# Attention, then a mixture of experts, on one core: choosing and turning the second slot of tokens earlier

## The chip, the core and the metric

The kernel runs on one core of a Trainium2 chip. The metric is device time in microseconds (us), the median of repeated runs. The engines are TensorE (PE; its weight loads are PEld), VectorE (DVE), ScalarE (ACT), GpSimd (POOL) and SyncE (SP). SP and POOL issue the DMAs.

## The reference

Eight batches of attention with twelve heads, 448 positions and a head of 64, scores capped by a tanh, in float32; then every token (3584 rows of 768) goes through the one of eight experts that its gate chooses.

```
scores = q @ k^T / sqrt(64)
scores = cap * tanh(scores / cap)
attn = softmax(scores)                    # over keys, with + 1e-9 in the sum
x = (attn @ v), heads side by side        # 3584 x 768
logits = x @ w_gate + modality_bias[modality_id]
e = argmax(logits, axis=1)
gate = softmax(logits)[e]
out[tokens of e] = gate * (relu(x @ w1[e]) @ w2[e])     # 768 -> 1024 -> 768
```

With the inputs as the reference draws them, expert 3 gets 1551 tokens (all of them in the first seven batches), expert 7 gets 1788 (1566 in the first seven) and expert 1 gets 245 (19); the others get none.

## The kernel before

*Attention.* The work is cut into 24 units of four heads, three to a batch, and each unit into seven steps of 64 keys. A step's scores are four matmuls; ScalarE takes tanh and exp; VectorE adds the exponentials up (tot); four more matmuls weigh v with them (xT). After a unit VectorE turns the result in blocks of 32 by 32 into token rows (tokens), and after a batch the rows, not yet divided by the softmax's sum, are stored to xd in device memory (store). Each row lies there in four quarters of 192 numbers.

*Routing.* After a batch, route finds each token's expert (oh), ranks it among its expert's tokens with two small matmuls (rank, from oh and from the running counts acc), and writes one entry of 16 numbers per token with indirect DMAs from POOL to the map, mapd, at row `expert * RG + rank` (L331). The entry holds the token, its gate weight, and two sets of six reciprocals of the softmax sums, each with the number of the row's quarter.

*Slots.* The experts' work is done in slots of 384 tokens (W) of one expert. A slot needs the expert's weights, its 384 map entries, and the rows that they name, gathered from xd into xg. The weights are float32 and are each split into a rounded part and the rest: ScalarE casts (ah, bh), VectorE subtracts (al, bl, L963), and each product is three matmuls. x is split in the same way (take, L987 and L988). A weight is loaded in blocks of 128 rows, through four buffers (raw) that are free again when VectorE has subtracted; w1 has six blocks, w2 eight.

*The first slot* is chosen from the counts after seven batches (early_slot): the first expert with at least 384 tokens. It is gathered, scaled and turned while the last batch is computed, and its first product is written out by hand together with the last batch's routing: hooks of ffn1 run after each block k and each column block f. The hook at ("k", 3) computes the last logits, the one at ("f", 3) ranks the last tokens, stores the last batch, and calls order().

*The other slots* are planned by slots() in order(), from the counts of all batches: a table (metai, copied to metad) with the expert and the map row of each full slot, and plani, which says how the rest ends. All of this is small VectorE instructions. FIXED planned slots run straight through; then one of four endings for the remainders.

*How a slot's x is made.* From the third slot on, quarter_rows reads the map in a layout in which each 32 partitions hold one quarter, quarter_index makes the row numbers (at), quarter_gather issues twelve indirect DMAs, and turn_rows lets VectorE scale and turn each 128 tokens into xt; take then splits xt. The second slot goes another way: rows() reads the map from SP as soon as metai is there, gather() issues three indirect DMAs, norm (L939) scales on VectorE, and TensorE turns xg by 18 transposes (move, L979) among the products of the first slot's ffn2.

What sets the order: instructions under pin keep the order of the program on their engine; the others are placed by the scheduler among them. Each engine works its row in order, so an instruction that waits holds up what stands behind it. In the first slot's ffn2 the products of the first 128 tokens go through the eight blocks of w2 once, both halves of a block together, and need bh and bl of that block.

Of the kernel before, what the change touches and what calls it, by code (L numbers as in the profile page):

```python
# [39 lines left out]
F32 = mybir.dt.float32  # L40
# [19 lines left out]
W = 384  # L60
# [12 lines left out]
FIXED = 7  # L73
# [18 lines left out]
class Program:  # L92
# [258 lines left out]
    def early_slot(self, pool, ps):  # L351

        nc = self.nc
        cnt = self.counts(pool, ps)
        sc = pool.tile([128, E], F32, name="esc")
        nc.vector.scalar_tensor_tensor(sc, cnt, float(W), self.desc, op0=ALU.is_ge, op1=ALU.mult)
        top = pool.tile([128, 1], F32, name="etop")
        nc.vector.tensor_reduce(top, sc, axis=AX.X, op=ALU.max)
        self.early = pool.tile([128, E], F32, name="early")
        nc.vector.tensor_scalar(self.early, sc, top, None, op0=ALU.is_equal)  # L360
        meta = pool.tile([128, 2], I32, name="emeta")
        for i, scale in enumerate((1.0, float(RG))):
            nc.vector.tensor_scalar(meta[:, i : i + 1], top, -scale, E * scale, op0=ALU.mult, op1=ALU.add)
        return meta

    def slots(self, pool, ps, early, then=None):
# [26 lines left out]
        if early:  # L393
            V.tensor_tensor(mask[:, :, 0], mask[:, :, 0], self.early, op=ALU.subtract)
            V.tensor_tensor(nbig, nbig, self.early, op=ALU.subtract)
# [6 lines left out]
        if early:  # L402
            V.tensor_tensor(start, base[:, :E], self.early, op=ALU.subtract)
        else:
            V.tensor_copy(start, base[:, :E])
# [76 lines left out]
    def attention(self, firsts, rp, xp):  # L482
        tc, nc = self.tc, self.nc
        pe, pin, V = nc.tensor, self.pin, nc.vector
        with ExitStack() as st:
# [330 lines left out]
            def last_ready():  # L816
                ready(5)
                turn2(SOON + 1)
                logits(SOON + 1)
                logits(SOON + 2)  # L820

# [15 lines left out]
            def last_rank():  # L837
                next(self.way, None)
                tokens(ND - 1)
                store(B - 1)  # L840
                soon(1)
# [47 lines left out]
    def quarter_rows(self, row, after=None):  # L889

        nc = self.nc
        r = self.register(nc.gpsimd, self.meta[row : row + 1, 1:2], NOROW, after)
# [29 lines left out]
    def quarter_gather(self, maps, n=TW):  # L922

        for g in range(n * 128 // FT):
            got = self.nc.gpsimd.indirect_dma_start(  # L925
                self.xg.rearrange("p t f -> p (t f)")[:, g * QW : (g + 1) * QW], None,
                self.xd.rearrange("n (q c) -> (n q) c", q=Q),
                bass.IndirectOffsetOnAxis(ap=maps[2][:, g : g + 1], axis=0),
                bounds_check=Q * NT - 1, oob_is_err=False,
# [306 lines left out]
    def run_slot(self, cur, n, ahead=None, raws=(), hooks=None, rows=None, few=False, index=None):  # L1236
# [24 lines left out]
        if hooks:  # L1261
# [3 lines left out]
            nxt[0], [lambda t=t: self.norm(nxt[1], t) for t in range(TW)] if hooks else (), quarters=bool(hooks)  # L1265
        )
        if nxt:
            if not hooks:
                for turn in turns:
                    turn()  # L1270
                then()
            pool = lambda k: (self.ps_h, "ph") if k % 3 == 2 else (self.ps_t, "ptr")
            moves = [
                lambda k=k: self.transpose(k, *pool(k)) if hooks else self.take(k, self.xt[:, k], nxt[2])
                for k in range(KC)
            ]
            if index:
                moves.insert(3, index)
# [5 lines left out]
    def run_slots(self, cur, hooks):  # L1284
# [4 lines left out]
        def rows(i, n=TW, more=True):  # L1289
            got = self.quarter_gather(maps[i], n)  # L1290
            if more:
                maps[i + 1] = self.quarter_rows(i + 1, got.ins)
# [6 lines left out]
        def ahead(i, n=TW):  # L1299
            if i == 0:  # L1300
                maps[0] = self.second
                maps[1] = self.quarter_rows(1, self.got)
            return self.expert(self.meta, i), maps[i], n

        for i in range(FIXED + 1):
            if i == FIXED:
                which = nc.values_load(self.plani[0:1, 2:3], min_val=0, max_val=len(ENDS))
            cur = self.run_slot(
                cur, TW, lambda: ahead(i), *((self.raws, hooks) if i == 0 else ()), rows=(lambda: rows(i)) if i else None,
                index=lambda: index(i + 1),  # L1310
# [143 lines left out]
    def build(self):  # L1454
        tc, nc = self.tc, self.nc
        with ExitStack() as st:
# [4 lines left out]
            with ExitStack() as sa:  # L1461
# [8 lines left out]
                with tc.If(big == 0) as branch:  # L1470
                    with ExitStack() as sb:
# [9 lines left out]
                        def order():  # L1481
                            self.meta = self.slots(rt, self.ps_r, True, hooks["last"])
                            self.second = self.rows(self.meta, 0)
                            self.got = self.gather(self.second).ins
# [68 lines left out]
```

## Time and profile before

| | |
|---|---|
| timed runs, median (three) | 802.48 us (800.44 to 803.19) |
| profiled execution, its own time | 795.47 us |
| its span, first to last instruction | 793.9 us |
| TensorE busy | 779.5 us, 98% |
| VectorE busy | 523.1 us, 66% |
| ScalarE busy | 502.2 us, 63% |
| POOL busy | 226.7 us, 29% |
| granted TensorE clock, mean | 0.998 of full |

The span begins with the first instruction and ends with the last; times in the rows below count from its start. Matmuls overlap in the pipeline, so a row's duration is longer than its distance to the next start. "Idle before" in square brackets is the time for which an engine waited ahead of an instruction, with what released it. Attention fills the first 300 us, the first slot's products run from 303 to 360 us, and the second slot starts there.

### The profile page before, as it was taken

Reading aid. Unit: us, or ns where it says so; the run is one execution under the profiler, and the core shown is the slowest. Engines: PE = TensorE matmul, PEld = TensorE weight load, DVE = VectorE, ACT = ScalarE, POOL = GpSimd, SP = SyncE. Lnnn points to the kernel's source line nnn. Section 1 sums busy time; section 2 is a strip of 40 time slices with the busy share of each in tenths; the row PEclk is TensorE's granted clock in tenths of the full one; section 3 lists DMA queues with packets and bytes.
Section 4 is the critical chain, followed back from the end, with each engine's and each line's share of the span. In section 5 each row is a group of like instructions: output and inputs, shape, how many; then the busy total and the mean of one; then the engine's idle time right before and its main releaser. Section 6 shows DMA issues by size and latency. Waiting matters only on the chain. (4 is left out here: it accounts for less than half of the span.)

```text
span 793.9 us, 15329 instructions
## 1 busy us (share of the span) xinstructions
PE 779.5 (98%) x5844; PEld 585.8 (74%) x5844; DVE 523.1 (66%) x875; ACT 502.2 (63%) x622; POOL 226.7 (29%) x258
## 2 busy tenths in 40 slices
PE   7999999999999999999999999999999999999996
PEld 3333333333333337999999999999999999999986
DVE  4688897888798898965826548265482664727830
ACT  6999999999999996354523545335443353537721
POOL 3000220022021150248180551814508146015202
PEclk9999999999999999999999999999999999999999
DMA  5466544362635565597445563465634645346772
GB/s 177 135 195 201 167 145 150 131 211 76 206 111 171 146 196 191 137 312 260 136 144 197 183 207 134 147 214 178 200 129 149 229 158 190 122 163 206 274 263 80
DMA packets 58787, 139.33 MB, mean 176 GB/s; under 512 B 9121, under 2 KB 25663, under 8 KB 58704
## 3 DMA queue, kind: packets, MB, share of 16 engines
q1 hardware_dynamic: 48224, 113.34, 44.1%
q0 software_dynamic: 10336, 24.91, 9.5%
q8 instruction: 48, 0.79, 0.4%
q14 instruction: 35, 0.29, 0.1%
q10 hardware_dynamic: 144, 0.00, 0.0%
HBM read 114.47 MB, written 24.34 MB: 175 GB/s over the span
## 5 line engine op out<-in xcount | busy, mean ns | idle before, releaser
L963 DVE TENSOR_TENSOR bl<-raw,bh 128x768 fp32r<-128x768 f32 x78 | 72.3, 956 | 121.8 <-ACT bh L962 120.6
L549 PE MATMUL xT<-pt,va 64*64 64x448 f32 x1344 | 151.5, 536 | 1.1 <-DVE xT L556 1.1
L521 ACT ACTIVATE pt<-sc 128x896 f32<-128x896 f32 x164 | 142.6, 906 | 10.4 <-PE sc L516 10.3
L1076 PE MATMUL py<-bh,hh 128*128 128x384 f32 x440 | 148.9, 339 | 0.1
L1076 PE MATMUL py<-bl,hh 128*128 128x384 f32 x440 | 148.3, 337 | 0.0
L1076 PE MATMUL py<-bh,hl 128*128 128x384 f32 x440 | 148.3, 337 | 0.0
L925 POOL DMA_INDIRECT xg<-xd,at x92 | 107.1, 1164 | 142.3 <-DVE at L908 114.0
L1022 PE MATMUL ph<-x,al 128*128 128x384 f32 (+1 forms) x456 | 147.3, 323 | 0.0
L524 ACT ACTIVATE pt<-pt 128x1792 f32<-128x1792 f32 x84 | 142.7, 1699 | 2.7
L537 DVE TENSOR_TENSOR tot<-tot,pt 128x896 f32<-128x896 f32 x118 | 127.9, 1084 | 11.0 <-ACT pt L524 6.4
L1018 PE MATMUL ph<-x,ah 128*128 128x384 f32 x360 | 120.6, 335 | 0.0
L1019 PE MATMUL ph<-x,ah 128*128 128x384 f32 x360 | 120.3, 334 | 0.0
L549 PEld LDWEIGHTS xT<-pt,va 64*64 64x64 f32 x1344 | 51.1, 133 | 76.2 <-issue 70.8
L331 POOL DMA_INDIRECT mapd<-pay,pos x32 | 36.3, 1134 | 233.4 <-DVE pos L324 185.8
L1098 ACT ACTIVATE ot<-py,mt 128x384 f32<-128x384 f32 x55 | 31.9, 580 | 107.4 <-PE py L1076 94.6
L1022 PEld LDWEIGHTS ph<-x,al 128*128 128x128 f32 x456 | 85.7, 188 | 0.0
L1033 ACT ACTIVATE hh<-ph 128x384 fp32r<-128x384 f32 x63 | 30.7, 491 | 85.3 <-PE ph L1022 81.4
L1076 PEld LDWEIGHTS py<-bh,hh 128*128 128x128 f32 x440 | 82.6, 188 | 1.0 <-ACT ot L1098 0.5
L516 PE MATMUL sc<-kq 64*64 64x448 f32 x672 | 79.5, 547 | 3.7 <-ACT pt L521 2.6
L1076 PEld LDWEIGHTS py<-bh,hl 128*128 128x128 f32 x440 | 82.6, 188 | 0.0
L1076 PEld LDWEIGHTS py<-bl,hh 128*128 128x128 f32 x440 | 82.6, 188 | 0.0
L516 PE MATMUL sc<-kx 64*64 64x448 f32 x672 | 78.6, 540 | 0.8 <-ACT pt L521 0.8
(248 smaller groups left out, 981.5 us busy)
## 6 DMA issues: line engine op xcount, KB each, us to landing
raw<-in_w_dram SPq DMA_DIRECT2D x81, 384.0 KB, 4.7
raw<-in_w_dram SPq DMA_DIRECT2D x48, 512.0 KB, 4.7
kq<-in_kq_dram SPq DMA_DIRECT2D x24, 448.0 KB, 4.2
va<-in_v_dram SPq DMA_DIRECT2D x24, 448.0 KB, 6.0
kx<-in_kq_dram SPq DMA_DIRECT2D x24, 448.0 KB, 4.0
xd<-xs SPq DMA_DIRECT2D x32, 336.0 KB, 7.1
raw<-in_w1q_dram SPq DMA_DIRECT2D x12, 512.0 KB, 6.5
mapd<-spare SPq DMA_DIRECT2D x4, 480.0 KB, 6.9
```

The costliest lines, as they stand in the source:

```text
L331: put = nc.gpsimd.indirect_dma_start(self.mapd, bass.IndirectOffsetOnAxis(ap=pos[:, c : c + 1], axis=0), pay[:, c, :], None, bounds_check= ...
L516: pin(pe.matmul(sc[i * KB : (i + 1) * KB, j, :S], kq[rows, s * KB : (s + 1) * KB], kq[rows, S:QK], start=True, stop=True,))
L521: pin(nc.scalar.activation(weights(n), sc[:, :, :S], AF.Tanh, scale=self.isc if slow else self.iscr))
L524: pin(nc.scalar.activation(pt, pt, AF.Exp, scale=self.cabsr))
L537: pin(V.tensor_tensor(tots[d], pt_of(n - 1) if s == 1 else tots[d], pt_of(n), op=ALU.add))
L549: pin(pe.matmul(self.xT[j * D : (j + 1) * D, i, :S], vas[d][rows, o : o + D], pt[rows, j], start=s == 0, stop=s == STEPS - 1,))
L925: got = self.nc.gpsimd.indirect_dma_start(self.xg.rearrange("p t f -> p (t f)")[:, g * QW : (g + 1) * QW], None, self.xd.rearrange("n (q c ...
L963: keep((minus or self.nc.vector).tensor_tensor(lo, raw, hi, op=ALU.subtract))
L1018: keep(nc.tensor.matmul(ph[:, :w], hi[:, fs], self.x[:, k, 0, :w], start=first, stop=False))
L1019: keep(nc.tensor.matmul(ph[:, :w], hi[:, fs], self.x[:, k, 1, :w], start=False, stop=False))
L1022: keep(nc.tensor.matmul(ph[:, :w], lo[:, fs], self.x[:, k, 0, :w], start=False, stop=last))
L1076: nc.tensor.matmul(pys[half][:, :HALF], self.h[a][:, f, rows], self.w2s[f][c][:, cs], start=f == i == 0, stop=f == FC - 1 and i == 2,)
```

## The change

One planned slot less (FIXED = 6), and a second slot that is chosen like the first one, from seven batches' counts: second_slot takes the first expert that still has 384 tokens when the first slot's are subtracted, which may be the same expert (both) and then means its second 384 map rows. This is done in the hook at ("k", 3). Its map rows are read there by POOL in the layout of quarters; in the hook at ("f", 3) the index is made and the twelve gathers are issued, from the first seven batches' rows of xd alone. VectorE scales and turns the rows between the differences of w1 (turn_rows in the place of norm), TensorE's transposes are gone, and w1 comes in the row order that the other slots use. slots() leaves out the two slots that are taken. The sums gone and some in slots() need no new counts, so the scheduler puts them where one and both are ready.

```diff
-FIXED = 7
+FIXED = 6
...
+    def second_slot(self, pool):
+        V, pin, early = self.nc.vector, self.pin, self.early
+        tile = lambda name, n, dt=F32: pool.tile([128, n], dt, name=name)
+        left, can, sc, top = tile("left2", E), tile("can2", E), tile("sc2", E), tile("top2", 1)
+        pin(V.scalar_tensor_tensor(left, early, -float(W), self.cnt, op0=ALU.mult, op1=ALU.add))
+        pin(V.tensor_scalar(can, left, float(W), None, op0=ALU.is_ge))
+        pin(V.tensor_tensor(sc, can, self.desc, op=ALU.mult))
+        pin(V.tensor_reduce(top, sc, axis=AX.X, op=ALU.max))
+        one, both, same, row = tile("one2", E), tile("both2", E), tile("same2", 1), tile("row2", 1)
+        pin(V.scalar_tensor_tensor(one, sc, top, can, op0=ALU.is_equal, op1=ALU.mult))
+        pin(V.tensor_tensor(both, one, early, op=ALU.mult))
+        pin(V.tensor_reduce(same, both, axis=AX.X, op=ALU.add))
+        pin(V.tensor_scalar(row, top, -float(RG), float(NOROW), op0=ALU.mult, op1=ALU.add))
+        meta = tile("emeta2", 2, I32)
+        pin(V.scalar_tensor_tensor(meta[:, 1:2], same, float(W), row, op0=ALU.mult, op1=ALU.add))
+        pin(V.tensor_scalar(top, top, -1.0, float(E), op0=ALU.mult, op1=ALU.add))
+        pin(V.tensor_scalar(meta[:, 0:1], top, float(E - 1), None, op0=ALU.min))
+        self.taken = one, both
+        return meta
...
-            V.tensor_tensor(mask[:, :, 0], mask[:, :, 0], self.early, op=ALU.subtract)
-            V.tensor_tensor(nbig, nbig, self.early, op=ALU.subtract)
+            one, both = self.taken
+            gone, some = tile("gone", [128, E]), tile("some", [128, E])
+            V.tensor_tensor(gone, self.early, one, op=ALU.add)
+            V.tensor_tensor(some, gone, both, op=ALU.subtract)
+            V.tensor_tensor(mask[:, :, 0], mask[:, :, 0], some, op=ALU.subtract)
+            V.tensor_tensor(mask[:, :, 1], mask[:, :, 1], both, op=ALU.subtract)
+            V.tensor_tensor(nbig, nbig, gone, op=ALU.subtract)
...
                 logits(SOON + 2)
+                meta = self.second_slot(self.cpool)
+                self.second = [meta, self.quarter_rows(meta, 0)]
...
             def last_rank():
                 next(self.way, None)
+                self.quarter_index(self.second[1])
+                self.got = self.quarter_gather(self.second[1], known=NT - S).ins
                 tokens(ND - 1)
...
-            nxt[0], [lambda t=t: self.norm(nxt[1], t) for t in range(TW)] if hooks else (), quarters=bool(hooks)
+            nxt[0], [lambda t=t: self.turn_rows(nxt[1], t) for t in range(TW)] if hooks else ()
...
-            pool = lambda k: (self.ps_h, "ph") if k % 3 == 2 else (self.ps_t, "ptr")
-            moves = [
-                lambda k=k: self.transpose(k, *pool(k)) if hooks else self.take(k, self.xt[:, k], nxt[2])
-                for k in range(KC)
-            ]
+            moves = [lambda k=k: self.take(k, self.xt[:, k], nxt[2]) for k in range(KC)]
...
-                            self.second = self.rows(self.meta, 0)
-                            self.got = self.gather(self.second).ins
```

Line numbers of the changed kernel are 26 to 30 higher than those of the kernel before. The rows of an engine show how the change moves instructions. First VectorE's row at the hook ("k", 3), behind the logits (lg) of the two last units but one; bl is the difference of w2's block 0, pay holds the reciprocals of the last unit. Before:

```order
L630 TENSOR_TENSOR lg<-lt,pay_3282 112x4x16 x4
L963 TENSOR_TENSOR bl_3171<-raw,bh_3170 128x768
L616 COPY pay_3282<-py 112x4x2x2
L617 TENSOR_TENSOR pay_3282<-pay_3282,py 112x4x2x2
L619 RECIPROCAL pay_3282<-pay_3282 112x4x2x2
L630 TENSOR_TENSOR lg<-py,pay_3282 112x4x16 x2
L271 TENSOR_REDUCE L<-lg 112x32
```

and in the changed kernel:

```order
L656 TENSOR_TENSOR lg<-lt,pay_3282 112x4x16 x4
L371 SCALAR_TENSOR_TENSOR left_3293<-early,cnt 128x8
L372 TENSOR_SCALAR can_3294<-left_3293 128x8
L373 TENSOR_TENSOR sc_3295<-can_3294,desc 128x8
L374 TENSOR_REDUCE top_3296<-sc_3295 128x1
L376 SCALAR_TENSOR_TENSOR one_3301<-sc_3295,top_3296,can_3294 128x8
L377 TENSOR_TENSOR both_3302<-one_3301,early 128x8
L417 TENSOR_TENSOR gone<-early,one_3301 128x8
L378 TENSOR_REDUCE same_3303<-both_3302 128x1
L379 TENSOR_SCALAR row_3304<-top_3296 128x1
L418 TENSOR_TENSOR some<-gone,both_3302 128x8
L381 SCALAR_TENSOR_TENSOR emeta_3309<-same_3303,row_3304 128x1
```

Two more of second_slot (L382, L383) and then bl and the copy into pay follow there: thirteen instructions now stand between lg and bl. Next TensorE's row at the rank product, where ptr and ph are sums of the first slot's first product (x with the parts ah and al of w1), before:

```order
L1022 MATMUL ptr<-x,al_175 128x384
L311 LDWEIGHTS tri
L311 MATMUL rank<-oh,tri 112x32
L1018 MATMUL ph<-x,ah_164 128x384
L1019 MATMUL ph<-x,ah_164 128x384
L1022 MATMUL ph<-x,al_165 128x384
L313 LDWEIGHTS ones
L313 MATMUL rank<-before,ones 112x32
```

and in the changed kernel:

```order
L1048 MATMUL ph<-x,ah_168 128x384
L1049 MATMUL ph<-x,ah_168 128x384
L1052 MATMUL ph<-x,al_169 128x384
L1048 MATMUL ph<-x,ah_170 128x384
L1049 MATMUL ph<-x,ah_170 128x384
L311 LDWEIGHTS tri
L311 MATMUL rank<-oh,tri 112x32
L1052 MATMUL ph<-x,al_171 128x384
L1048 MATMUL ph<-x,ah_172 128x384
L313 LDWEIGHTS ones
L313 MATMUL rank<-before,ones 112x32
L1049 MATMUL ph<-x,ah_172 128x384
```

The two matmuls of rank (and the counts behind them) stand eleven matmuls of 128x384 further back; six of the eleven stand ahead of the first row shown. Last VectorE's row at the differences of the second slot's w1 (al), before:

```order
L963 TENSOR_TENSOR al_167<-raw,ah_166 128x1024
L939 TENSOR_TENSOR xg<-xg,mt 128x384 x2
L963 TENSOR_TENSOR al_169<-raw,ah_168 128x1024
L939 TENSOR_TENSOR xg<-xg,mt 128x384 x2
L963 TENSOR_TENSOR al_171<-raw,ah_170 128x1024
L939 TENSOR_TENSOR xg<-xg,mt 128x384 x2
L963 TENSOR_TENSOR al_173<-raw,ah_172 128x1024
L963 TENSOR_TENSOR al_175<-raw,ah_174 128x1024
L988 TENSOR_TENSOR x<-ptr,x 128x384 x3
```

and in the changed kernel:

```order
L993 TENSOR_TENSOR al_167<-raw,ah_166 128x1024
L976 TENSOR_TENSOR xg<-xg,win 128x768
L977 STREAM_TRANSPOSE xt<-xg 128x4x6x32
L993 TENSOR_TENSOR al_169<-raw,ah_168 128x1024
L976 TENSOR_TENSOR xg<-xg,win 128x768
L977 STREAM_TRANSPOSE xt<-xg 128x4x6x32
L993 TENSOR_TENSOR al_171<-raw,ah_170 128x1024
L976 TENSOR_TENSOR xg<-xg,win 128x768
L977 STREAM_TRANSPOSE xt<-xg 128x4x6x32
L993 TENSOR_TENSOR al_173<-raw,ah_172 128x1024
L993 TENSOR_TENSOR al_175<-raw,ah_174 128x1024
L1018 TENSOR_TENSOR x<-xt,x 128x384 x3
```

Each pair of scalings (xg<-xg,mt) has become one scaling and one turn into xt, and the takes read xt where they read the transposes' ptr.

## Rows read from the trace of the kernel before

**Rows 1.** Table of stretches: span, busy us of PE, PEld, DVE, ACT, POOL.

```profile
core 0: us, PE busy (x) PEld busy (x) DVE busy (x) ACT busy (x) POOL busy (x), PEclk, DMA share, GB/s
310.00:320.00 10.00, 9.94 (x63) 9.44 (x60) 7.69 (x30) 4.10 (x9) 0.00 (x0) 1.00 0.12 41
320.00:330.00 10.00, 10.00 (x59) 9.84 (x59) 9.49 (x44) 3.20 (x6) 3.89 (x4) 1.00 0.58 119
330.00:340.00 10.00, 10.00 (x59) 10.00 (x58) 8.39 (x29) 3.76 (x5) 2.22 (x3) 1.00 0.82 236
```

**Rows 2.** TensorE's timeline around the transposes: start, us, engine, line, operation, tiles, count.

```profile
349.04 0.34 PE L1076 MATMUL py<-bh,hl 128*128 128x384 f32 x1
...
350.38 0.98 PE L979 MATMUL ptr<-ident,xg 128*128 128x128 f32 x7 [0.78 <-DVE xg L939]
...
351.38 0.33 PE L1076 MATMUL py<-bl,hh 128*128 128x384 f32 x1
...
355.25 0.34 PE L1076 MATMUL py<-bh,hl 128*128 128x384 f32 x1
...
356.59 0.33 PE L1076 MATMUL py<-bl,hh 128*128 128x384 f32 x1
```

**Rows 3.** VectorE's timeline where the change inserts, and small instructions.

```profile
313.25 0.95 DVE L963 TENSOR_TENSOR bl<-raw,bh 128x768 fp32r<-128x768 f32 x1
314.36 0.18 DVE L616 COPY pay<-py 112x16 f32<-112x16 f32 x1 [0.15 <-PE py L579]
...
318.60 0.19 DVE L296 TENSOR_REDUCE first<-sc 112x4 f32<-112x32 f32 x1
318.82 0.19 DVE L298 TENSOR_TENSOR oh<-sc,first 112x32 bf16<-112x32 f32 x1
...
325.31 0.17 DVE L392 SCALAR_TENSOR_TENSOR rowt<-nbig,region 128x8 f32<-128x8 f32 x1
325.39 0.17 DVE L394 TENSOR_TENSOR mask<-mask,early 128x8 f32<-128x8 f32 x1
```

**Rows 4.** VectorE's timeline, end of the plan and behind it.

```profile
334.67 0.16 DVE L473 CAST plani<-plan 1x3 int32<-1x3 f32 x1
334.94 3.81 DVE L963 TENSOR_TENSOR bl<-raw,bh 128x768 fp32r<-128x768 f32 x4
```

**Rows 5.** TensorE's timeline: rank product, block 4 of w2, second slot's start.

```profile
318.67 0.34 PE L1022 MATMUL ptr<-x,al 128*128 128x384 f32 x1
319.07 0.22 PE L311 MATMUL rank<-oh,tri 112*112 112x32 bf16 x1
...
336.51 0.34 PE L1076 MATMUL py<-bl,hh 128*128 128x384 f32 x1
336.68 0.34 PE L1076 MATMUL py<-bh,hl 128*128 128x384 f32 x1
...
360.63 0.34 PE L1018 MATMUL ph<-x,ah 128*128 128x384 f32 x1
```

**Rows 6.** ScalarE's timeline, blocks 6 and 7 of w2.

```profile
335.93 1.82 ACT L962 CAST bh<-raw 128x768 fp32r<-128x768 f32 x2 [1.54 <-DMA raw<-in_w_dram]
```

**Rows 7.** DMA issues in 332-332.6, 343-343.6 and 358-376: us to landing.

```profile
raw<-in_w_dram SPq DMA_DIRECT2D x1, 384.0 KB, 4.6
...
raw<-in_w1q_dram SPq DMA_DIRECT2D x1, 512.0 KB, 7.3
...
raw<-in_w_dram SPq DMA_DIRECT2D x4, 384.0 KB, 4.7
```

**Rows 8.** POOL: the quarter gathers (min/median/max ns); one map write.

```profile
L925 POOL DMA_INDIRECT xg<-xd,at x92: 995/1002/2738, 356.7 to 725.8; - x92
...
322.99 1.04 POOL L331 DMA_INDIRECT mapd<-pay,pos  x1 [27.24 <-issue]
```

**Rows 9.** VectorE's timeline: a later slot's turn; two differences of w1.

```profile
377.45 0.95 DVE L946 TENSOR_TENSOR xg<-xg,win 128x768 f32<-128x768 f32 x1
378.44 0.98 DVE L947 STREAM_TRANSPOSE xt<-xg 128x768 f32<-128x768 f32 x1
...
342.14 2.36 DVE L963 TENSOR_TENSOR al<-raw,ah 128x1024 fp32r<-128x1024 f32 x2 [3.40 <-ACT ah L962]
```

More of the change, by code (lines that the diff above doesn't have):

```diff
@@ L353, in early_slot @@
         nc = self.nc
-        cnt = self.counts(pool, ps)
+        cnt = self.cnt = self.counts(pool, ps)
         sc = pool.tile([128, E], F32, name="esc")
@@ L402, in slots @@
         if early:
-            V.tensor_tensor(start, base[:, :E], self.early, op=ALU.subtract)
+            V.tensor_tensor(start, base[:, :E], gone, op=ALU.subtract)
         else:
@@ L887, in rows, with quarter_rows @@
         return mt
-    def quarter_rows(self, row, after=None):
+    def quarter_rows(self, meta, row, after=None):
         nc = self.nc
-        r = self.register(nc.gpsimd, self.meta[row : row + 1, 1:2], NOROW, after)
+        r = self.register(nc.gpsimd, meta[row : row + 1, 1:2], NOROW, after)
         win = self.mp.tile([128, W // FT, SEG], F32, name="win", bufs=2)
@@ L920, in gather, with quarter_gather @@
         return got
-    def quarter_gather(self, maps, n=TW):
+    def quarter_gather(self, maps, n=TW, known=NT):
         for g in range(n * 128 // FT):
@@ L926, in quarter_gather @@
                 self.xg.rearrange("p t f -> p (t f)")[:, g * QW : (g + 1) * QW], None,
-                self.xd.rearrange("n (q c) -> (n q) c", q=Q),
+                self.xd[:known].rearrange("n (q c) -> (n q) c", q=Q),
                 bass.IndirectOffsetOnAxis(ap=maps[2][:, g : g + 1], axis=0),
-                bounds_check=Q * NT - 1, oob_is_err=False,
+                bounds_check=Q * known - 1, oob_is_err=False,
             )
@@ L1291, in rows @@
             if more:
-                maps[i + 1] = self.quarter_rows(i + 1, got.ins)
+                maps[i + 1] = self.quarter_rows(self.meta, i + 1, got.ins)
             if i == FIXED + 1:
@@ L1299, in ahead @@
         def ahead(i, n=TW):
-            if i == 0:
-                maps[0] = self.second
-                maps[1] = self.quarter_rows(1, self.got)
+            if i < 0:
+                maps[0] = self.quarter_rows(self.meta, 0, self.got)
+                return self.expert(self.second[0], 0), self.second[1], n
             return self.expert(self.meta, i), maps[i], n
-        for i in range(FIXED + 1):
+        for i in range(-1, FIXED + 1):
             if i == FIXED:
@@ L1308, in run_slots @@
             cur = self.run_slot(
-                cur, TW, lambda: ahead(i), *((self.raws, hooks) if i == 0 else ()), rows=(lambda: rows(i)) if i else None,
-                index=lambda: index(i + 1),
+                cur, TW, lambda: ahead(i), *((self.raws, hooks) if i < 0 else ()),
+                rows=(lambda: rows(i)) if i >= 0 else None, index=lambda: index(i + 1),
             )
```

## Prediction

> **What bounds the kernel now.** The page comes first: TensorE is busy for 98% of the span, so the time changes by what is added to or taken from TensorE's stream, and by nothing else. The change lies between 310 and 362 us, in and right behind the first slot, so the table of stretches is the second view: there TensorE has no room, its granted clock is full (1.00), and VectorE, at 9.49 and 8.39 of 10 us, is nearly as full as TensorE from 320 to 340 us [rows 1]. The third view is TensorE's timeline around the second slot's turns. Eighteen 128x128 transposes stand in its stream, in two groups of nine, and the first group waits 0.78 us for VectorE's L939 [rows 2]. Last come the timelines of VectorE and TensorE side by side, from which one sees how long before its use each weight of the first slot's second product is ready [rows 3 to 5].
>
> **What is removed: 3.0 us of TensorE's stream.** The matmuls of 128x384 start 0.17 us apart [rows 5]. From the last product ahead of the first group of transposes to the second one behind it are 351.38 - 349.04 = 2.34 us where two steps would be 0.34: 2.00 us, the wait of 0.78 in them. Around the second group it is 356.59 - 355.25 - 0.34 = 1.00 us [rows 2]. Both go, since the takes L988 now read xt, which VectorE fills. Everything behind is one dense stream up to the last slots, so these 3.0 us come off the end, unless they are given back ahead of it.
>
> **What is added ahead of it: VectorE is later.** Into VectorE's row, behind the logits at 313.2 us and ahead of bl, come thirteen small instructions (second_slot, and the two sums gone and some), later one quarter index, and in slots one more subtraction: fifteen. The trace shows two prices for their kind: 0.22 us where one needs the result of the one in front (318.60 to 318.82), 0.08 us where it does not (325.31 to 325.39) [rows 3]. Some nine of the fifteen need the one in front: 9 x 0.22 + 6 x 0.08 = 2.5 us; the 0.15 us for which VectorE idles there today swallows as much of it [rows 3]. I take 2.3 us; the bounds are all fifteen at 0.08 less 0.15, 1.05 us, and all at 0.22 less 0.15, 3.15 us. From there to the copy of plani VectorE has next to no idle time [rows 1], and the four differences bl of w2 blocks 4 to 7 stand right behind that copy in the same row [rows 4]; so they come 2.3 us later.
>
> The Trainium skill, page "VectorE: DVE Perf Modes", section "The DRAIN you can't avoid", says that every Vector instruction flushes its pipeline before the next one starts, so that the count of instructions is what costs. The rows do not bear this out for instructions that do not need each other: they last 0.17 us and start 0.08 us apart [rows 3]. [...]
>
> Who waits for that: TensorE uses the first of these four (block 4) at 336.51 [rows 5]; it is ready at 334.94 + 3.81/4 = 335.89 [rows 4]. That is 0.62 us of room. With 2.3 us of delay TensorE waits 2.3 - 0.62 = 1.7 us (0.4 to 2.5 by the bounds). The rank product is a second such place: oh comes later by the same amount, plus a hidden difference hl that now stands in front of it; in TensorE's row the rank product is moved eleven matmuls back, 1.9 us, against some 2.3 + 0.5 for oh. Today 318.67 to 319.07 is one step of 0.17 and 0.23 of wait [rows 5]; it becomes about 0.6. That is not added: what TensorE loses there, it does not wait again at block 4.
>
> **What is added beside it: transfers.** Blocks 6 and 7 of w2 are loaded into the buffers that bl of blocks 2 and 3 free, and ScalarE already waits for block 6 (1.54 us) today; its bh starts as the load lands [rows 6]. That load is issued 2.3 us later too, which the 1.7 above contains, and it now runs beside the twelve quarter gathers, which start behind the four map writes, at about 330 us, and not only once the plan is made. If it takes longer, TensorE waits that much longer. Today such a load lands in 4.6 us here; in the stretch where a later slot's twelve gathers run, in 4.7; at the worst place, beside three gathers and six loads, a larger one took 7.3 [rows 7]. So 0 to 2.7 us; nearest is the 4.7, but here the store of the last batch runs as well: I take 0.5.
>
> **What costs nothing.** POOL's five map reads at about 316 us stand ahead of the four map writes, which must wait for them to land; the first write starts at 322.99 today [rows 8] and, with VectorE later, at about 325, so the reads have 6 us after their issue. The twelve gathers need no store of the last batch (they read the first seven batches' rows) and no plan; at 1.0 us each and some 0.3 between [rows 8] they are issued by 346 us. VectorE turns the first tile after two differences al, at about 347, so it does not wait for them. SP reads no map row any more and fetches the expert's number early; the w1 loads still wait for bl to free their buffers. Behind POOL's gathers stand metad, the next map reads and the first output store: they come behind 346 us, and the next slot's index is wanted only at about 358.
>
> The turns are more VectorE work: three pairs of 0.95 and 0.98 us [rows 9] in the place of six scalings. Is VectorE late for the second slot's first product then? With bl ending at 341.5, six al (2.36 for two [rows 9]) and three pairs, the first take follows at about 358, and the first product starts at 360.63 - 0.8 [rows 5]. Some 1.8 us of room are left, and the further takes come as fast (0.5 us) as the product uses them (three steps of 0.17). So this stays hidden; it is what is late next.
>
> **The sum.** -3.0 + 1.7 + 0.5 = -0.8 us. The profiled execution took 795.47 us (a span of 793.9 and 1.6 around it); it becomes 794.7. That execution lies 7 us under the median of the timed runs, 802.48; a shift of TensorE's stream carries over as it is, so 801.7.
>
> **Rivals.**
> - *The whole gain.* VectorE's delay is below the room of 0.62 plus what the schedule absorbs, and TensorE keeps its pace: -3.0 or a little less, 799.5 us. For it: instructions that overlap at 0.08 us. Against: the chain from left to top is serial, and even the lower bound exceeds the room.
> - *The gain is more than given back.* The loads of w2 blocks 6 and 7 are squeezed between the last batch's store and the gathers. For it: the DMA engines are at 0.82 already in 330 to 340 us [rows 1], and 7.3 us was seen when gathers and loads met [rows 7]. Against: the 4.7 us with twelve gathers. From a landing of 4.6 + 1.3 = 5.9 us it decides; at 7.3 the sum is -3.0 + 1.7 + 2.7 = +1.4, 803.9 us, and with VectorE at its upper bound +2.2, 804.7. Slower than before by more than that needs longer landings still.
> - *POOL is held up.* Twelve gathers are to be prepared while VectorE is at its fullest. The slowest of 92 took 2.74 us [rows 8]; at that price each, with 0.3 between, they end at 330 + 36 = 366, land by 369, and after turn and take the second slot starts at about 372 instead of 360: +11 us, 813. Against: the usual one takes 1.0, and a map write beside a VectorE at 9.49 of 10 took 1.04 [rows 1, 8]. The Trainium skill, page "SBUF — State Buffer", section "SBUF: two separate sides", has this as a rule: VectorE and GpSimd share a port pair by an exclusive lock, and a VectorE instruction in a two-port mode, or with two SBUF inputs against a GpSimd one that reads SBUF, keeps GpSimd from writing descriptors until it ends. In these rows the lock does not show.
> - *The second choice finds nothing.* Then the slot is blank and its work is done one slot later: 288 matmuls at 0.174 us, +50 us, 852. By the reference's own inputs seven batches give experts 3 and 7 some 1550 tokens each, so the second slot is the second 384 rows of expert 3, the same rows as the planner takes today.
>
> **How the numbers follow.** Forecast (TensorE gives back 0.4 to 3.4 of the 3 us) 0.59; whole gain 0.19; given back with interest 0.17; POOL 0.04; blank 0.01. The forecast's own range is -2.6 (lower bounds, 799.9) to +0.4 (upper delay and 0.9 for the transfers, 802.9). A measurement of this kernel tells 0.3% (2.4 us) from no change: below 800.1 lie the whole gain and a bit of the forecast's low end, 0.22; above 804.9 the upper part of the third case, POOL and the blank slot, and some scatter of the runs, 0.17; 0.61 remain. For 8 in 10 I take 799.3 to 804.8.
>
> **What would show it.** After the change: no transposes of xg from 345 us on; TensorE waiting for bl of L963 (its new line) around 338 us, 1 to 2.5 us in total, and for oh at the rank product about 0.6; bl of block 4 at about 337.2; twelve gathers on POOL between 330 and 346 at 1.0 us each; the second slot's first product at about 359.8 with no wait for a take. I am wrong if TensorE shows no wait at block 4, if ScalarE's wait for block 6 is over 2.5 us, or if a take or a gather holds the second slot.

## The result, and the profile after

| | before | changed |
|---|---|---|
| timed runs, median (six each) | 802.78 us (800.44 to 804.48) | 811.16 us (808.74 to 813.03) |
| ratio | | 1.0101 (95%: 1.0076 to 1.0126) |
| profiled execution: span | 793.9 us | 809.7 us |
| TensorE busy | 779.5 us, 98% | 781.9 us, 97% |
| granted TensorE clock, mean | 0.998 | 0.991 |

Slower by 1.0% where 801.7 us was predicted. The table of stretches of the changed kernel, to be laid beside [rows 1] (the columns are the same, and the last four are granted clock, DMA share and GB/s):

```profile
330.00:340.00 10.00, 10.00 (x59) 10.00 (x59) 8.95 (x40) 0.98 (x2) 7.38 (x8) 1.00 0.81 163
340.00:350.00 10.00, 2.45 (x14) 2.13 (x12) 1.48 (x10) 1.75 (x3) 7.87 (x8) 0.73 0.58 196
350.00:360.00 10.00, 7.13 (x25) 6.30 (x25) 4.98 (x16) 2.56 (x5) 5.08 (x8) 0.59 0.57 155
```

TensorE stands still for most of 340 to 350 us, and its clock is then granted at half (1.2 of 2.4 GHz, from 344.5 to 358.2 us). Where it stands, in its own timeline:

```profile
337.46 0.34 PE L1052 MATMUL ph<-x,al 128*128 128x384 f32 x1
...
341.62 0.34 PE L1106 MATMUL py<-bh,hl 128*128 128x384 f32 x1
349.51 1.01 PE L1106 MATMUL py<-bh,hh 128*128 128x384 f32 x2 [7.55 <-ACT hh L1063]
353.24 0.69 PE L1106 MATMUL py<-bl,hh 128*128 128x384 f32 x1 [2.72 <-DVE bl L993]
```

The first row is the last product of hidden block 7 (column block f = 7) of the first slot; it ends at 337.8. TensorE then runs through w2 blocks 0 to 3 and waits 7.55 us, by the view for ScalarE's hh of block 7, and then 2.72 for bl. ScalarE's timeline:

```profile
334.71 0.49 ACT L1063 ACTIVATE hh<-ph 128x384 fp32r<-128x384 f32 x1 [2.63 <-PE ph L1052]
348.25 0.49 ACT L1063 ACTIVATE hh<-ph 128x384 fp32r<-128x384 f32 x1 [13.05 <-remote]
348.63 3.02 ACT L992 CAST bh<-raw 128x768 fp32r<-128x768 f32 x4
```

hh of block 7 needs only that product, and starts 10.4 us behind it. "remote" says that the view found no instruction that ended this wait. What TensorE's next product needs is bh of w2 block 4, the first of the four casts, which stands right behind hh in ScalarE's row: it ends at 349.45, and TensorE goes on at 349.51. VectorE stood behind hh (8.48 us), and its plan and bl of block 4 [rows 4] came only then:

```profile
348.77 0.56 DVE L1064 SCALAR_TENSOR_TENSOR hl<-ph,hh 128x384 fp32r<-128x384 f32 x1 [8.48 <-ACT hh L1063]
...
351.79 0.34 DVE L499 CAST plani<-plan 1x3 int32<-1x3 f32 x1 [0.58 <-issue]
352.06 1.83 DVE L993 TENSOR_TENSOR bl<-raw,bh 128x768 fp32r<-128x768 f32 x2
```

Meanwhile POOL issues the new gathers, twelve of them, right behind the map writes:

```profile
334.35 0.94 POOL L331 DMA_INDIRECT mapd<-pay,pos  x1 [0.31 <-issue]
335.60 1.06 POOL L955 DMA_INDIRECT xg<-xd,at  x1 [0.30 <-issue]
...
350.51 0.99 POOL L955 DMA_INDIRECT xg<-xd,at  x1 [0.30 <-issue]
```

Below the views, the trace keeps the times at which semaphores were updated; by such an update an engine signals that an instruction is done. Of block 7's products, the last one of each of the six row blocks signals. In the profile of before TensorE's updates stand 0.52 us apart there, as do the products. In the changed kernel's they come at 336.12, 338.97, 341.84, 345.40 and 348.23 us, five for six products, and the last of these, 0.02 us ahead of hh, lets ScalarE go. The Trainium skill, page "Perfetto Trace Analysis", section "Summary: the profiler window per engine type", says that the spreading of a signal lies outside the time that a row shows, for TensorE too; this trace agrees, with 10.4 us of it behind a row that ends at 337.8, a size that the page does not give. I count a signal of TensorE, VectorE or ScalarE as late when the trace has no update within 0.06 us of its instruction's end, and ask whether POOL was issuing a transfer at that time (or up to 0.4 us behind it; the usual gap between two issues is 0.3). An update that the trace lacks counts as late too: the changed kernel's profile has 774 updates for 846 signals of VectorE, that of before 832 for 832.

```
profile of            POOL issuing      otherwise
before                1 of 638 late     0 of 1602
changed             252 of 649 late     0 of 1594
```

So signals were late in the profiled run of the changed kernel, only while POOL issued, and in that of before not at all, but for one. Theory S: where signals are late, twelve issues in a row hold TensorE's signals of block 7. Rivals: R, an accident of this one run; V, VectorE's new instructions; D, the transfers themselves.

### The profile page after: what moved, and what is told of

The parts are those of the page before. It is cut to its first block, busy times and chain, and to the rows that moved or that the text cites. A ratio compares the mean times of both kernels' runs of the same rounds, so it can differ in the third digit from the quotient of the medians.

```text
span 809.7 us, 15337 instructions
## 1 busy us (share of the span) xinstructions
PE 781.9 (97%) x5826; PEld 584.1 (72%) x5826; DVE 525.2 (65%) x890; ACT 500.9 (62%) x622; POOL 242.9 (30%) x272
## 5 line engine op out<-in xcount | busy, mean ns | idle before, releaser
L955 POOL DMA_INDIRECT xg<-xd,at x104 | 121.0, 1163 | 146.6 <-DVE at L938 116.2
L992 ACT CAST bh<-raw 128x768 fp32r<-128x768 f32 x78 | 62.2, 832 | 24.8 <-DMA raw<-in_w_dram 23.2
```

Of the source, the lines that this page charges most:

```text
L955: got = self.nc.gpsimd.indirect_dma_start(self.xg.rearrange("p t f -> p (t f)")[:, g * QW : (g + 1) * QW], None, self.xd[:known].rearrange ...
L992: keep((cast.tensor_copy if cast else self.nc.scalar.copy)(hi, raw))
```

## Experiments

Ratios are to the kernel before, measured beside it on the same chip.

**Both kernels again** (no edit).

> The changed kernel once more. Theory S (signals): while POOL issues twelve gathers in a row, TensorE's signals to ScalarE get through late, so the hidden block 7 of the first slot (hh of L1063) starts some 10 us after its product, as at 348.25 us in the first profile; every run must show it: hh of block 7 held 8 to 12 us, TensorE's two waits at L1106 about 10 us, the granted clock at half for about 13 us behind it, 809 to 813 us. Rival R (one run): the hold is an accident of the profiled run, and this profile shows hh of block 7 within 1 us of its product and no fall of the clock.

> The kernel before once more, as a second look at it, since its first profile (795.5 us) lay 7 us under its median. Theory S: no hold of hh of block 7 (its twelve gathers start a slot later), TensorE's signals on time at 325 to 340 us; what the first profile lacked against the median, some 6 to 7 us, stands ahead of 310 us, as ScalarE's and TensorE's waits in the attention stage (7.2 us in 13 waits in the changed kernel's profile, 3.4 in 4 in the first of before). Rival R: holds of several us come and go in this kernel too.

Measured: before 796.16 us (21 runs) and its copy 0.9999 (0.9989 to 1.0009); changed 792.64, ratio 0.9957 (0.9940 to 0.9974). Here the change makes the kernel faster, and in the changed kernel's profile at most one signal in some 710 is late. S as written had the hold in every run: wrong. hh of block 7 starts as its product ends, and of TensorE's waits the two for bl are those that the prediction named:

```profile
337.83 0.45 PE L1106 MATMUL py<-bl,hh 128*128 128x384 f32 x1 [1.10 <-DVE bl L993]
340.32 0.44 PE L1106 MATMUL py<-bl,hh 128*128 128x384 f32 x1 [0.30 <-DVE bl L993]
342.65 0.44 PE L1106 MATMUL py<-bh,hh 128*128 128x384 f32 x1 [0.15 <-ACT ot L1128]
```

**The gathers later; row gathers**, beside the runs above. The first issues the twelve gathers in order(), behind slots() and the write of metad, and no longer in the hook at ("f", 3):

```diff
-        nc.gpsimd.dma_start(self.metad, metai)
+        self.metaput = nc.gpsimd.dma_start(self.metad, metai).ins
...
-                self.got = self.quarter_gather(self.second[1], known=NT - S).ins
...
+                            with self.tc.issue_after(self.metaput):
+                                self.got = self.quarter_gather(self.second[1], known=NT - S).ins
```

> The changed kernel with the twelve quarter gathers issued behind the write of metad, about 3 to 4 us later (from about 339 us in place of 335.6), so that the product of block 7 is over when the first is issued; all else as it is. Theory S: hh of block 7 starts within 1 us of its product, TensorE's wait there (7.6 us) goes, 800 to 803 us. Rival D (data: it is the transfers of the gathers, the loads and the store together that are too much, wherever the gathers stand): the hold only moves, to bl or to the casts of w2 blocks 4 to 7, and 807 us or more remain. Rival V (VectorE's fifteen instructions are the loss): unchanged at 809 to 813.

The second keeps the early choice and fetches whole rows by three gathers; row_map is one read of the map by POOL:

```diff
-                self.second = [meta, self.quarter_rows(meta, 0)]
+                self.second = [meta, self.row_map(meta, 0)]
...
-                self.quarter_index(self.second[1])
-                self.got = self.quarter_gather(self.second[1], known=NT - S).ins
+                self.got = self.gather(self.second[1], known=NT - S).ins
```

norm and the transposes are as in the kernel before.

> The changed kernel with the early choice and one planned slot less, but the second slot's rows fetched by three whole-row gathers and turned by TensorE (eighteen transposes), as in the kernel before. Theory S: three gathers do not hold the signals, hh of block 7 is on time; time as before plus VectorE's delay, 802 to 805 us. Rival V (the early choice's instructions on VectorE are the loss): 809 us or more. Rival D: in between, 804 to 808, since the gathers still run beside the loads.

Measured: 0.9969 (0.9952 to 0.9986) and 0.9990 (0.9981 to 1.0000). With signals on time neither tells S from V or D. The second does show that the early choice alone gains nothing measurable.

**The plan's arithmetic behind bl.** plan() is the arithmetic from plan to plani, taken out of slots().

```diff
             self.load_w2(cur[0], raws, range(W2_EARLY, FC))
+            self.plan()
             nxt = ahead()
```

> The changed kernel with the eighteen small VectorE instructions that work out the number of the ending (plan to plani) moved behind the four differences bl of w2 blocks 4 to 7; their order alone is changed. By the prediction's own step (VectorE late for bl of block 4) TensorE's wait for bl at L1106 (1.10 + 0.30 us in the second profile of the changed kernel) falls to under 0.5 us and the time lies 1 us under that of the changed kernel beside the same before: ratio 0.994 to 0.996 where the runs of before are near 796 us. Theory S (signals late while POOL issues) on a chip where before takes 800 us or more: the wait of hh of block 7 stays and the kernel is slower than before by 5 us or more. Rival D (loads): bl of block 4 waits for its load instead and nothing is gained.

Measured: 0.9950 (0.9933 to 0.9967), signals on time. TensorE's wait for bl fell to 0.38 + 0.27 us (under 0.5 was expected), as the prediction's step wants. The 0.75 us that this saves are too little to tell the time from the changed kernel's.

**Only the turns; the changed kernel a third time**, side by side. The first has turn_rows in the place of norm and of the transposes, as in the changed kernel, and makes index and gathers in ahead(0):

```diff
-                            self.second = self.rows(self.meta, 0)
-                            self.got = self.gather(self.second).ins
+                            self.second = self.quarter_rows(0)
```

> The kernel before with only the gathering and turning changed: the second slot is still chosen by the plan of all eight batches, its rows gathered in quarters and turned by VectorE, nothing is computed early on VectorE. The eighteen transposes leave TensorE, and no instruction of second_slot delays bl. If the early choice is only a price (VectorE's 2 us) and the turns alone bring the gain: 3 us faster than before. My theory: the map's five reads can start only behind the plan's number, the twelve gathers behind them (some 343 to 359 us), the turns behind those, so that TensorE waits for the second slot's rows: slower than before by 5 to 12 us, with the wait at the first product of the second slot.

> The changed kernel a third time, beside the kernel before on the same chip. Theory S with a condition (signals between engines are late only on some chips or at some times, and there only while POOL issues transfers): where before takes about 796 us, this takes 792 to 793.5 and no signal is late; where before takes about 803 us, this takes 809 to 813, with hh of block 7 held 8 to 12 us. Rival R (an accident that can fall on either kernel at any time): 803 beside 796 or 793 beside 803.

Measured: 1.0090 (1.0067 to 1.0112) and 0.9943 (0.9921 to 0.9966). Without the early choice the rows come too late, as expected:

```profile
PE ph L1018 <- ACT x L987: 5.0, 1, 5.0
PE ph L1019 <- DVE x L988: 1.6, 1, 1.6
```

So the turns need the early choice, and together they gain what neither does alone.

**Both moves; the new tiles alone**, side by side.

> The changed kernel with both moves: the twelve gathers behind the write of metad, and the arithmetic of plani behind bl of w2 blocks 4 to 7. By the runs so far: TensorE's wait for bl 0.3 to 0.7 us (1.4 in the changed kernel, 0.65 with the plan moved, 1.0 with the gathers moved), ratio 0.994 to 0.997 where before takes 796 us. Theory S, where before takes 800 us or more: here no gather is issued until the product of block 7 is over, so hh of block 7 is held at most 2 us and the ratio stays under 1.003, against 1.010 for the changed kernel there.

```diff
                     meta = self.early_slot(self.cpool, self.ps_r)
+                    for name, n in (("left2", E), ("can2", E), ... ("emeta2", 2)):
+                        nc.gpsimd.memset(self.cpool.tile([128, n], F32, name=name), 0.0)
```

> The kernel before with the nine small tiles of second_slot laid into the pool of constants, and a fill of zeros on GpSimd for each; nothing else. The products of the later slots start 174.4 ns apart in before and 173.8 in the changed kernel (1720 matmuls between 400 and 700 us), which is worth 0.18 us a slot. If that comes from where the buffers lie in memory, this kernel shows 173.8 and is 1 to 1.5 us faster than before; if it comes from the order of the work, it shows 174.4 and is the same.

Measured: 0.9964 (0.9947 to 0.9982), no gain over the gathers' move alone, and TensorE waits 0.9 us for bl (0.3 to 0.7 was expected); and 0.9992 (0.9976 to 1.0007), products 174.2 ns apart, between the two values expected. Where the buffers lie explains at most a third of the closer products.

**The hold made by hand.**

```diff
+            if hooks and f == FC - 1:
+                keep = self.pin
+                peek = self.cpool.tile([128, 1], F32, name="peek")
+                keep(nc.scalar.copy(peek, self.xg.rearrange("p t f -> p (t f)")[:, 7 * QW : 7 * QW + 1]))
             keep(nc.scalar.activation(hh[:, f, :w], acc, AF.Relu))
```

> The changed kernel with ScalarE held in front of hh of block 7 by a copy of one column out of the eighth gathered quarter, which lands near 345.8 us in the second profile of the changed kernel; this does by hand what the late signal did in the first profile (hh started 10.4 us behind its product). If that one hold is what the change pays where signals are late: hh of block 7 starts some 10 us late, TensorE waits 7 to 10 us at L1106 for hh and 2 to 3 for bl, its granted clock falls to half for some 13 us, and the time is 8 to 11 us above the changed kernel on the same chip: 800.5 to 803.5 where before takes 796.5, a ratio of 1.005 to 1.009. Rival (the hold hides behind VectorE's plan or the loads): under 3 us more than the changed kernel, 792.5 to 795.5.

Measured: 802.56 us, ratio 1.0072 (1.0043 to 1.0100), 10 us above the changed kernel's 792.5 to 792.75 in three other comparisons. ScalarE's timeline and TensorE's waits:

```profile
342.26 0.19 ACT L1066 COPY peek<-xg 128x1 f32<-128x1 f32 x1 [12.68 <-DMA xg<-xd,at]
342.36 0.48 ACT L1067 ACTIVATE hh<-ph 128x384 fp32r<-128x384 f32 x1
```

```profile
PE py L1110 <- ACT bh L992: 7.3, 1, 7.3
PE py L1110 <- DVE bl L993: 2.0, 1, 2.0
```

The clock is at half from 340.5 to 350.7 us. Here the view names bh, which stands behind hh. One hold of hh of block 7, with signals on time, costs 10 us; between the changed kernel's ratio in the first comparison (1.0101) and with signals on time (0.9943 to 0.9957) lie some 12 us. In the first profile the parts are the two waits, 7.55 + 2.72 us, and some 2.8 us that eighteen matmuls lost at half the clock (0.32 us from start to start for 0.17), less the 1.4 us of wait with signals on time.

**To meet late signals again.** The same kernels, later:

> The changed kernel with the twelve gathers behind the write of metad, a second time, to meet a chip or a time at which signals are late. Where before takes about 796 us: 793 again, nothing new. Where before takes 800 us or more, theory S: the product of block 7 is over before the first gather, hh of block 7 is held at most 2 us, 801 to 806 us; rival D (the transfers): 809 or more, with the hold at the casts and differences of w2 blocks 4 to 7.

> The changed kernel with three row gathers and TensorE's transposes, a second time, for the same purpose. Where before takes about 796 us: 795.7 again. Where before takes 800 us or more, theory S: three gathers of 1 us in place of twelve hold the signals for under 4 us, hh of block 7 is not held, 802 to 805 us; rival V (VectorE's early instructions): 809 or more.

Measured: 0.9969 and 0.9994 beside 796.73 us; on time again. Then:

> The changed kernel a fourth time, at a later hour, to meet signals that are late again. Theory S with its condition: 792 to 793.5 where before takes about 796; 809 to 813 with hh of block 7 held 8 to 12 us where before takes about 803. Rival R (accident of a run): the pairs mix.

Measured: before 808.49 us, changed 818.72, ratio 1.0116 (1.0086 to 1.0146), and the hold is back:

```profile
334.02 0.49 ACT L1063 ACTIVATE hh<-ph 128x384 fp32r<-128x384 f32 x1 [2.63 <-issue]
348.49 0.49 ACT L1063 ACTIVATE hh<-ph 128x384 fp32r<-128x384 f32 x1 [13.98 <-remote]
```

The next three runs were on the chip of "Both kernels again", an hour later:

> The kernel before, profiled where signals are late (before 808, changed 819 us one call earlier). Theory S: VectorE's, ScalarE's and TensorE's signals late in the stretches in which GpSimd issues transfers here too (the map writes of the attention stage, the twelve gathers of each later slot), which costs it 6 to 12 us against 796, most of it as ScalarE's and TensorE's waits ahead of 310 us; in the first slot no hold of hh of block 7 over 2 us, and no fall of the clock. Rival R: signals on time, the extra time lies elsewhere.

> The changed kernel with the twelve gathers behind the write of metad, where signals are late. Theory S: the product of block 7 is over before the first gather, hh of block 7 is held at most 2 us, and the ratio to before falls from 1.0116 to 0.996 to 1.003. Rival D (the transfers, or gathers beside loads, wherever they stand): 1.008 or more, the hold at the casts and differences of w2 blocks 4 to 7.

> The changed kernel with three row gathers and TensorE's transposes, where signals are late. Theory S: three gathers in the place of twelve, issued ahead of the map writes, hold no signal of block 7: ratio 0.999 to 1.003. Rival V (the early choice's instructions on VectorE): 1.008 or more.

Measured, with before at 802.14 us (24 runs): the copy of before 1.0006 (0.9996 to 1.0017), the gathers later 0.9985 (0.9966 to 1.0004), row gathers 1.0060 (1.0029 to 1.0091). This chip had given 796.16 for before with its signals on time. Now:

```
profile of                     POOL issuing      otherwise
before (before_late)         218 of 620 late     2 of 1620
gathers later                232 of 669 late     2 of 1574
row gathers                  225 of 653 late     3 of 1602
changed (after_fourth)       240 of 649 late     2 of 1594
```

The kernel before has late signals too. But its POOL is silent when block 7 ends; POOL's timeline in that profile, and ScalarE's:

```profile
333.26 0.94 POOL L331 DMA_INDIRECT mapd<-pay,pos  x1 [0.30 <-issue]
337.18 0.59 POOL L436 DMA_DIRECT2D metad<-metai  x1 [2.98 <-DVE metai L435]
345.23 1.58 POOL L914 DMA_INDIRECT xg<-xd,mt  x1 [7.46 <-DMA raw<-in_w1q_dram]
```

```profile
338.60 0.49 ACT L1033 ACTIVATE hh<-ph 128x384 fp32r<-128x384 f32 x1 [2.63 <-PE ph L1022]
```

With the gathers later it is the same; POOL and ScalarE there:

```profile
334.09 0.94 POOL L331 DMA_INDIRECT mapd<-pay,pos  x1 [0.30 <-issue]
338.00 0.60 POOL L462 DMA_DIRECT2D metad<-metai  x1 [2.96 <-DVE metai L461]
338.91 1.45 POOL L954 DMA_INDIRECT xg<-xd,at  x1 [0.30 <-issue]
```

```profile
337.56 0.49 ACT L1062 ACTIVATE hh<-ph 128x384 fp32r<-128x384 f32 x1 [2.63 <-PE ph L1051]
```

The same transfers, issued some 4 us later, beside the same VectorE work, and the loss is gone: S, against V and D. The row gathers missed S's number (0.999 to 1.003): I had not seen that the three gathers, ahead of the map writes, push these back to 336.05 us, into the signals of blocks 6 and 7. POOL's last map write and ScalarE's hh:

```profile
335.10 0.95 POOL L331 DMA_INDIRECT mapd<-pay,pos  x1 [0.30 <-issue]
```

```profile
332.41 0.49 ACT L1068 ACTIVATE hh<-ph 128x384 fp32r<-128x384 f32 x1 [2.63 <-issue]
337.09 0.49 ACT L1068 ACTIVATE hh<-ph 128x384 fp32r<-128x384 f32 x1 [4.19 <-PE ph L1057]
```

hh of block 6 is 1.6 us late, and four updates of TensorE arrive together at 337.07 to 337.24, 1.0 us behind the end of that write. TensorE then waits for bl, and its clock is at half from 345.6 to 349.1 us, as in the first profile but shorter:

```profile
345.37 0.48 PE L1111 MATMUL py<-bl,hh 128*128 128x384 f32 x1 [2.01 <-DVE bl L998]
```

With signals on time this kernel waited 1.5 us for bl, so the wait is 0.5 us longer here, and the slower clock costs some 1.7 us by its starts 0.32 us apart. That is 2.2 of the 5.6 us between its ratios, 1.0060 and 0.9990; where the rest is, no run shows.

**Last**, the changed kernel and both moves, meant for a time with late signals:

> The changed kernel at an hour at which signals are late (one call earlier before took 802.1 us on a chip that had given 796.2 an hour before). Theory S: ratio 1.008 to 1.014, hh of block 7 held 8 to 13 us; by theory R (a matter of the chip of the first comparison) 0.994 to 0.997 on another chip.

> The changed kernel with the gathers behind the write of metad and plani's arithmetic behind bl of w2 blocks 4 to 7, at an hour at which signals are late. Theory S: ratio 0.996 to 1.001, as with the gathers' move alone (0.9985); if VectorE's order matters more where signals are late, under 0.996.

Measured: before 796.43 us, signals on time; 0.9944 (0.9928 to 0.9961) and 0.9968 (0.9956 to 0.9980). So the changed kernel and the one with the gathers later were not run beside each other where signals are late.

## Why the prediction was wrong

*The step that failed* is the one on the gathers under "What costs nothing": "The twelve gathers need no store of the last batch ... and no plan; at 1.0 us each and some 0.3 between [rows 8] they are issued by 346 us". The issue was right to two us (330.0 to 347.7 us in the second profile of the changed kernel); its price was taken as transfers alone, 0.5 us. I asked who waits for the gathers, and not whose signals pass while POOL issues them. Where signals are late, twelve issues lie across the signals of block 7: hh 10.4 us late, TensorE's waits of 7.55 + 2.72 us, and the clock at half behind them.

*Removed, 3.0 us, and VectorE's delay, 1.7 us:* right in kind where signals are on time. The transposes and their 0.78 us of wait are gone [rows 2]; the thirteen instructions take from 313.42 to 315.40 us, 2.0 us (2.3 taken with two more), 0.15 us each. The section of the Trainium skill that was weighed there (page "VectorE: DVE Perf Modes", section "The DRAIN you can't avoid") also says "A next op that is not held starts earlier", which the prediction leaves out. The trace agrees with that much: starts lie 0.06 to 0.12 us apart where an instruction does not need the one in front, and 0.18 to 0.27 where it does. The waits at bl are 1.10 + 0.30 for 1.7 + 0.5. At the second slot's first outputs the changed kernel is 1.3 us ahead of before in the second pair of profiles, for the 0.8 of the sum. The rank product waits 0.2 us for oh, not 0.6; by the prediction's own terms it would be 0.23 + 2.8 - 1.9 = 1.1. Nor does its first take at 358 us follow from its terms (341.5 + 7.1 + 5.8 = 354.4); it came at 356.85. Neither is part of the sum.

*What the sum lacked there:* the products of the later slots start 173.8 ns apart, for 174.4 before (means over some 1720 between 400 and 700 us): 288 x 0.6 ns = 0.18 us a slot, 1.3 us over seven. The row gathers' kernel has it, the one with only the turns (174.4) has not, so it comes with the early choice's half of the change; tiles alone gave 174.2. What makes it stays open. With it the span is 2.7 us shorter, and the three comparisons with signals on time give 3.5 to 4.8 us by their medians. The whole gain (799.5 us) was the nearest rival there, by another way than its own.

*The shift to the timed runs* hid the sign of it. The profile of before lay 7 us under the median, and I carried a difference over without asking what the 7 us were. They fit late signals: where profiles showed these, before took 802 to 808 us, on time 796. Of the first comparison's timed runs of before no trace shows it. One place where they go in before is TensorE's wait for ScalarE in attention, where POOL writes the map; the first row is from the second profile of before, the second from before_late (columns: us in total, times, longest):

```profile
PE sc L516 <- ACT pt L521: 3.4, 4, 1.6
```

```profile
PE sc L516 <- ACT pt L521: 6.7, 12, 1.6
```

*The rivals:* "POOL is held up" (0.04) did not decide, since no take or gather held the second slot; what cost the time is that POOL held the others. But POOL was held a little, and there the prediction misread its rows ("the lock does not show"). Of the twelve gathers five took 1.2 to 1.75 us in the second profile of the changed kernel, and one 1.50 in the first. POOL's and VectorE's timelines in the second:

```profile
338.95 1.00 POOL L955 DMA_INDIRECT xg<-xd,at  x1 [0.30 <-issue]
340.25 1.75 POOL L955 DMA_INDIRECT xg<-xd,at  x1 [0.30 <-issue]
```

```profile
339.31 1.83 DVE L993 TENSOR_TENSOR bl<-raw,bh 128x768 fp32r<-128x768 f32 x2 [0.66 <-ACT bh L992]
```

Each of the five ends 0.87 us behind the end of a bl or al, VectorE's differences of two inputs in SBUF. In the profile of before 18 of 92 gathers took over 1.15 us, the 2.74 of [rows 8] among them, all beside a VectorE instruction of two inputs that lasted over 0.3 us; of the 59 beside none not one did. This agrees with the rule that the prediction gives from the Trainium skill, page "SBUF — State Buffer", section "SBUF: two separate sides". The loads cost TensorE at most the second wait for bl, 0.30 us, and the second slot was not blank, which would have been some 50 us.

*Not settled:* why signals are late at one time and on time at another. It isn't fixed to the chip, one of which showed both an hour apart; no kernel of mine could bring it about.

## What to carry to other kernels

An instruction stream on GpSimd that issues many transfers in a row can cost the other engines their signals, even when nobody waits for the transfers; place it where no engine hangs on a fresh signal, which here took a few lines and a delay of some 4 us, and gave no loss where signals were late (0.9985) and a gain where they were on time (0.9969). A profile that lies several us beside the timed runs is a profile of another condition: find what the difference is made of before carrying a sum over. And a difference of 1% in one comparison can turn its sign in the next (1.0101 and 1.0116 against 0.9957, 0.9943 and 0.9944), so take it on more than one chip and at more than one time.

## What the hardware showed

- Signals of TensorE, VectorE and ScalarE were late in over a third of the cases while POOL issued a transfer (218 to 252 of 620 to 669), and at most in 3 of some 1600 otherwise, in five profiles; in the other fifteen 0 or 1 of some 640 to 720.
- TensorE's updates then came about one for each gather or two: 1.4 us apart in a later slot (575.24, 576.67, 578.08, 579.55 us), 2.8 to 3.6 in the first, and five within 0.2 us (580.96 to 581.14) some 1.6 us behind the end of the last gather, in the first profile of the changed kernel.
- In the first profile of the changed kernel the granted clock fell to half during TensorE's standstill of 7.55 us and came back while it worked without a gap; in the row gathers' kernel it fell behind a standstill of 2.01 us (345.6 to 349.1); in the kernel before, with late signals but no such standstill, it never fell before the end.
- A gather that POOL issued beside a VectorE instruction with two inputs in SBUF could take longer than the usual 1.0 us, up to 2.74 in the kernel before; in the second profile of the changed kernel the five longer ones of the first slot ended 0.87 us behind the end of a bl or al.
